# Pooled attention and a maxout layer on one core: five batches' keys turned by DMA, their copies on another engine, two schedules shifted

## The chip, the cores and the metric

The kernel runs on one core of a Trainium2 chip. The metric is the device time of one execution in microseconds, as a median over runs. The core's engines are TensorE (PE; its weight loads are listed apart as PEld), VectorE (DVE), ScalarE (ACT), GpSimd (POOL) and SyncE (SP). SP's work here is issuing DMAs; POOL and ACT can issue some as well. Each engine takes its instructions in program order and waits where a semaphore tells it to.

## The reference

```python
# attention with pooled keys and values: 8 batches, 8 heads, 576 rows, 64 columns
k_p = k.reshape(B, H, Sp, pool, D).mean(axis=3)      # pool = 8, Sp = 72
v_p = v.reshape(B, H, Sp, pool, D).mean(axis=3)
scores = np.matmul(q, k_p.transpose(0, 1, 3, 2)) / np.sqrt(D)
attn = softmax(scores)                               # over the 72 pooled keys
x = matmul(attn, v_p).transpose(0, 2, 1, 3).reshape(4608, 512)
# maxout layer
h = np.maximum(np.maximum(x @ w1, x @ w2), x @ w3)   # 512 -> 768
out = h @ w_out                                      # 768 -> 512
```

## The kernel before

The 4608 tokens are worked off in nine blocks of 512 (`block`, L432). A block has slots. A slot of `hidden_part` (L289) is one of three weight matrices for one block `jc` of 128 hidden columns: four matmuls into a PSUM tile `pw` (three buffers), which is then emptied: the first by a cast on ACT (L301), the second by a maximum on DVE (L304), the third by a maximum on DVE that writes hT (L307). Six column blocks make 18 slots. Four slots of `project` (L323) follow, each six matmuls for 128 tokens, a copy from PSUM to `osb` (five buffers) and two stores.

Between the slots stands the attention of a later batch. What comes after which slot is written out by hand: for block 0 in the dictionary at L447, for the others in `plan` (L456), and `do` (L258) carries the steps out. Block n works on batch n + 1:

- `T`: the queries are transposed into `qT` by one DMA transpose on SP's queue (L270), a block ahead. `q`/`Q` do it on PE, with the copy on ACT or DVE.
- `k` (`turn_k`, L183): the pooled keys `kp` are transposed by six PE transposes into one PSUM tile `pkt` (L174), and two copies (L179) spread them into the zero-padded `kz`, one for even heads and one for odd ones. `a` and `K` pool batch 1's keys.
- `s0` to `s7`: the scores of a head, three matmuls (L203), and their exponential on ACT (L208).
- `v0` to `v4`: a chunk of 128 tokens, eight matmuls (L238), then a reciprocal and a product on DVE (L244, L246) that give `xn`.
- `x0` to `x4`: such a chunk is transposed into `xT`, the input of `hidden_part`: by PE and a copy (L229, L233) for batches 0 and 1, by a DMA transpose on SP's queue (L223) from batch 2 on. `X` puts the copy on DVE.

Loading and pooling run on POOL: `pool_work` (L467), after the first slot of block n, issues the loads of k, q and v of batch n + 2 and adds groups of eight rows up into `kp` and `vp`. The load of k is bound to the end of the block's first group of matmuls.

As blocks 0 and 1 begin while the values of their tokens are still being worked out, `hidden` (L311) cuts their first column blocks into parts of 128 or 256 tokens.

SP's queue is the order in which the program issues: transposes `T` and `x`, and the stores. The last tile's output is made in two halves of 256 columns: ACT empties the first, DVE the second, and each half's two stores go one to SP's queue and one to ACT's.

Of the kernel before, what the change touches and what calls it, by code (L numbers as in the profile page):

```python
# [14 lines left out]
def kernel(  # L15
# [11 lines left out]
    nc = tc.nc  # L27
    dt = mybir.dt
    F32, BF16, F16 = dt.float32, dt.bfloat16, dt.float16
# [13 lines left out]
    GS = (0, 2, 4, 6, 8, 1, 3, 5, 7)  # L43
    NR = 64
    KCH = C // 128
    JCH = DFF // 128
    TOK = B * S
    NB = 512
# [4 lines left out]
    sb2 = ctx.enter_context(tc.tile_pool(name="sb2", bufs=2))  # L53
# [1 line left out]
    psp = ctx.enter_context(tc.tile_pool(name="psp", bufs=1, space=PSUM))  # L55
    ctx.enter_context(tc.manual_schedule())

    kts, vts, qbs, kps, qTs, ets = {}, {}, {}, {}, {}, {}

    def after(loads, first):  # L60
        for x in loads:
# [49 lines left out]
    for i in range(3):  # L111
# [6 lines left out]
        out=wo_sb, in_=moe_w_out.rearrange("(jc p) c -> p jc c", p=128))  # L118
# [25 lines left out]
    def fold_k(b, e, i0=0, i1=6):  # L144
        if b not in kps:
            new_kp(b)
        fold(e, kts[b][:, i0:i1], [kps[b][:, i0:i1, i, :] for i in range(2)])
# [23 lines left out]
    def keys(b, tag):  # L171
        pkt = psp.tile([128, 6, 96], BF16, name="pkt", tag=tag[0], bufs=tag[1])
        for i in range(6):
            nc.tensor.transpose(pkt[:, i, :], kps[b][:, i, :, :], ident[0:96, 0:96])  # L174
        return pkt

    def fill_kz(b, par, h0, h1, pkt, evac):
        rows = slice(64 * par, 64 * par + 64)
        evac(out=kz_all[b % 2][rows, par, h0:h1, 0:Sp].rearrange(  # L179
                 "p h (r i) -> p h r i", i=6),  # L180
             in_=pkt[rows, :, 12 * h0:12 * h1].rearrange("p i (h r) -> p h r i", r=12))

    def turn_k(b):  # L183
        pkt = keys(b, TR)
        for par in range(2):
            fill_kz(b, par, 0, H, pkt,
                    nc.scalar.copy if b == 1 else nc.vector.tensor_copy)

    def pool_k(b, tag):

# [19 lines left out]
    def new_et(b):  # L210
        ets[b] = sb2.tile([Sp, H, S], F16, name="et", tag="et")
# [40 lines left out]
    TR = ("tr", 1)  # L252
# [5 lines left out]
    def do(b, steps):  # L258

        for name in steps.split():
            i = int(name[1:] or 0)
            if name[0] in "qQ":
                turn_q(b, *QS[i], nc.vector.tensor_copy if name[0] == "Q"
                       else nc.scalar.copy, TR)
            elif name[0] == "T":
                qTs[b] = sb2.tile([128, 2 * NG, 128], BF16, name="qT", tag="qT")
                nc.sync.dma_start_transpose(  # L270
                    out=qTs[b], in_=qbs[b].rearrange("p hp t d -> p (hp t d)"))
            elif name[0] == "k":
                turn_k(b)
            elif name[0] == "K":
                pool_k(b, PW)
            elif name[0] == "a":
                nc.vector.tensor_tensor(out=k16, in0=kts[b][:, :, 0:4],
                                        in1=kts[b][:, :, 4:8], op=ALU.add)
            elif name[0] == "s":
                if i == 0:  # L280
                    new_et(b)
                scores(b, i)
            elif name[0] == "v":
                xns[b, i] = values(b, CHUNKS[i][0])
            else:
                turn_x(b, *CHUNKS[i], xns[b, i], TR,
                       nc.vector.tensor_copy if name[0] == "X" else nc.scalar.copy)
# [23 lines left out]
    def hidden(n, hT):  # L311

        parts = [(0, JCH, 0, NB)]
        if n == 0:
            parts = [(0, 1, 0, 128), (0, 1, 128, 256), (1, 2, 0, 256), (0, 2, 256, NB),
                     (2, JCH, 0, NB)]
        elif n == 1:
            parts = [(0, 1, 0, 256), (0, 1, 256, NB), (1, JCH, 0, NB)]
        for j0, j1, c0, c1 in parts:
            for jc in range(j0, j1):  # L320
                yield from hidden_part(n, jc, c0, c1, hT)

    def project(n, hT):  # L323
        for mm in range(4):
            m = 4 * n + mm
            last = m == TOK // 128 - 1
            osb = sb3.tile([128, C], F32, name="osb", tag="osb", bufs=5)
            for c in ((slice(0, C // 2), slice(C // 2, C)) if last else (slice(0, C),)):
                po = psp.tile([128, c.stop - c.start], F32, name="po", tag="pw", bufs=3)
                for jc in range(JCH):  # L330
                    nc.tensor.matmul(po, hT[:, jc, bass.ts(mm, 128)], wo_sb[:, jc, c],  # L331
                                     start=(jc == 0), stop=(jc == JCH - 1))
                if c.start:
                    nc.vector.tensor_copy(out=osb[:, c], in_=po)
                else:
                    nc.scalar.copy(out=osb[:, c], in_=po)  # L336
                for u in range(2):
                    b, g = divmod(2 * m + u, NG)
                    dst = out[S * b:S * b + S, :].rearrange("(r g) c -> r g c", g=NG)
                    (nc.scalar if last and u else nc.sync).dma_start(  # L340
                        out=dst[:, GS[g], c], in_=osb[64 * u:64 * u + 64, c])
            yield

    def new_hT():
        return sb2.tile([128, JCH, NB], F16, name="hT", tag="hT")
# [13 lines left out]
    for i in range(0, 6, 2):  # L359
        src = kts[0][:, i:i + 2] if i else kt0  # L360
        f = const.tile([96, 2, 4, D], F32, name="kf", tag="kf")
# [5 lines left out]
            out=kps[0][:, i:i + 2].rearrange("p i a d -> p a i d"),  # L367
# [64 lines left out]
    def block(n, plan):  # L432

        hT = new_hT()
        slot = 0
        for part in (hidden(n, hT), project(n, hT)):
            for _ in part:
                if slot == 0 and n > 0:
                    pool_work(n, mms[-1])
                for b, steps in plan.get(slot, ()):  # L440
                    if b < B:
                        do(b, steps)
                slot += 1

    fold_v(1)
    fold_k(2, nc.gpsimd)
    block(0, {0: [(0, "X1")], 3: [(0, "v2")], 5: [(0, "v3")], 6: [(0, "x2")],  # L447
# [6 lines left out]


    def plan(n):  # L456
        b, i = n + 1, 3 * (n == 1)
        got = {0: [], 3: [], 3 + i: [(b, "k")]}
        got.update({5 + i + h: [(b, f"s{h}")] for h in range(H)})
        got[12 + i].append((b + 1, "T"))  # L460
        got.update({15 + i + c: [(b, f"v{c} x{c}")] for c in range(5)})
        if n == 1:
            got[0].append((1, "x3"))
            got[3].append((1, "x4"))
        return got
# [45 lines left out]
```

The softmax here doesn't subtract the row's maximum and nothing guards it: scores larger than these inputs give would overflow.

## Time and profile before

| | |
|---|---|
| median of 5 runs | 243.14 us (242.5 to 245.42) |
| profiled execution | 242.5 us, its span 240.7 us |
| PE busy | 231.5 us, 1609 matmuls |
| matmuls of the hidden layer (L295) | 696, 155.6 us |
| matmuls of the projection (L331) | 222, 50.7 us |
| key transposes on PE (L174), 96 columns | 54, mean 206 ns |
| copies to kz on DVE, 64x576 | 12, mean 755 ns |
| copies to kz on ACT, 64x576 | 2, mean 633 ns |
| DMA transposes to xT on SP's queue | 30, median 2.4 us to landing (2.3 to 7.9) |
| DMA transposes to qT on SP's queue | 6, median 6.6 us to landing (4.5 to 8.1) |

The span runs from the first to the last recorded instruction; the time of an execution also holds 1.8 us around it. In the timeline a row gives start, duration, engine, line, operation, tile written and tiles read, shape, count, and in brackets how long the engine was idle before it and what ended that. A matmul's duration goes from its start to the end of its last result, so successive matmuls overlap in the record and their pace is read from their starts. A "q" after an engine's name means its instruction queue, as for DMAs that it issues.

### The profile page before, as it was taken

Reading aid. Unit: us, or ns where it says so; the run is one execution under the profiler, and the core shown is the slowest. Engines: PE = TensorE matmul, PEld = TensorE weight load, DVE = VectorE, ACT = ScalarE, POOL = GpSimd, SP = SyncE. Lnnn points to the kernel's source line nnn. Section 1 sums busy time; section 2 is a strip of 40 time slices with the busy share of each in tenths; the row PEclk is TensorE's granted clock in tenths of the full one; section 3 lists DMA queues with packets and bytes.
Section 4 is the critical chain, followed back from the end, with each engine's and each line's share of the span. In section 5 each row is a group of like instructions: output and inputs, shape, how many; then the busy total and the mean of one; then the engine's idle time right before and its main releaser. Section 6 shows DMA issues by size and latency. Waiting matters only on the chain.

```text
span 240.7 us, 4221 instructions
## 1 busy us (share of the span) xinstructions
PE 231.5 (96%) x1609; PEld 123.0 (51%) x1609; DVE 131.6 (55%) x239; ACT 100.1 (42%) x173; POOL 123.7 (51%) x91
## 2 busy tenths in 40 slices
PE   7798999999999999999999999999999999999992
PEld 2477555575554555455545554555455544444441
DVE  6856754564574558354836483648364834504530
ACT  2373347546523651365135523552355232142121
POOL 8864265999997489557953787389200000000000
PEclk9999999999999999999999999999999999999999
DMA  7999999999958994799489967997530353042006
GB/s 138 181 198 206 194 200 210 182 160 245 156 128 148 218 198 91 133 229 204 102 151 186 186 146 143 213 184 130 121 87 0 69 124 83 3 109 66 0 20 154
DMA packets 51939, 34.29 MB, mean 142 GB/s; under 512 B 32144, under 2 KB 46480, under 8 KB 51920
## 3 DMA queue, kind: packets, MB, share of 16 engines
q0 software_dynamic: 17088, 17.11, 45.7%
q1 hardware_dynamic: 34672, 16.79, 33.3%
q8 instruction: 12, 0.20, 0.3%
q10 hardware_dynamic: 160, 0.13, 0.2%
q14 instruction: 7, 0.06, 0.1%
HBM read 34.60 MB, written 9.44 MB: 183 GB/s over the span
## 4 chain that ended last, share of the span: by engine, by line
PE 88%; DVE 5%; ACT 2%; DMA 2%; issue 1%; DVEq 0%
PE pw L295 55%; PE po L331 18%; PE psc L203 6%; PE pav L238 4%; DMA kt<-in_k_dram 2%; PE pxt L229 1%; DVE kf L362 1%; ACT et L208 1%; DMA out_dram<-osb 1%; DVE t L304 1%; PE pkt L174 1%; PE pvp L156 1%; DVE xn L246 1%; PE pqt L167 1%; DVE kp L366 1%
## 5 line engine op out<-in xcount | busy, mean ns | idle before, releaser
L295 PE MATMUL pw<-xT,mw 128*128 128x512 f16 (+2 forms) x696 | 155.6, 364 | 0.7 <-ACT xT L233 0.7
L295 PEld LDWEIGHTS <-mw 128*128 128x128 f16 x696 | 61.9, 98 | 56.1 <-issue 1.0
L304 DVE TENSOR_TENSOR t<-t,pw 128x512 f16<-128x512 f16 (+2 forms) x58 | 37.8, 651 | 71.0 <-PE pw L295 43.7
L301 ACT CAST t<-pw 128x512 f16<-128x512 f32 (+2 forms) x58 | 32.3, 556 | 56.1 <-PE pw L295 54.8
L331 PE MATMUL po<-mwo,hT 128*128 128x512 f16 (+1 forms) x222 | 50.7, 373 | 0.0
L208 ACT ACTIVATE et<-psc 72x576 f16<-72x576 f32 (+2 forms) x62 | 40.7, 662 | 20.9 <-PE psc L203 20.8
L307 DVE TENSOR_TENSOR hT<-t,pw 128x512 f16<-128x512 f16 (+2 forms) x58 | 37.7, 650 | 9.0 <-PE pw L295 5.3
L336 ACT COPY osb<-po 128x512 f32<-128x512 f32 (+1 forms) x36 | 20.9, 580 | 47.7 <-PE po L331 43.6
L135 POOL TENSOR_TENSOR half<-vt 72x2048 f32<-72x2048 f16 x7 | 28.4, 4060 | 7.0 <-DMA vt<-in_v_dram 6.9
L331 PEld LDWEIGHTS <-hT 128*128 128x128 f16 x222 | 20.3, 97 | 21.3 <-DVE hT L307 2.4
L135 POOL TENSOR_TENSOR half<-kt 96x1536 f32<-96x1536 f16 x6 | 18.5, 3084 | 21.2 <-DMA kt<-in_k_dram 21.2
L246 DVE TENSOR_TENSOR xn<-pav,rcp 128x512 f16<-128x512 f32 x39 | 27.0, 691 | 1.6 <-DVE rcp L244 0.2
L136 POOL TENSOR_TENSOR half<-half 72x1024 f32<-72x1024 f32 (+1 forms) x13 | 27.3, 2098 | 1.0
L203 PE MATMUL psc<-qT,kz 128*128 128x64 bf16 (+3 forms) x192 | 25.8, 246 | 0.4 <-DVE kz L179 0.3
L203 PEld LDWEIGHTS <-kz 128*128 128x128 bf16 x192 | 17.8, 98 | 15.6 <-DVE kz L179 1.5
L238 PEld LDWEIGHTS <-et 72*128 72x128 f16 x312 | 15.2, 98 | 7.6
L238 PE MATMUL pav<-vp,et 72*128 72x65 f16 x312 | 16.5, 194 | 0.0
L244 DVE RECIPROCAL rcp<-pav 128x8 f32<-128x8 f32 x39 | 7.9, 204 | 9.4 <-PE pav L238 9.3
L139 POOL TENSOR_TENSOR kp<-half 96x384 bf16<-96x384 f32 x12 | 11.7, 993 | 0.5
L179 DVE COPY kz<-pkt 64x576 bf16<-64x576 bf16 (+1 forms) x14 | 9.9, 711 | 2.9 <-PE pkt L174 2.7
L79 POOL DMA_DIRECT2D vt<-in_v_dram x10 | 8.0, 804 | 3.9 <-PE pw L295 2.9
L139 POOL TENSOR_TENSOR vp<-half 72x512 f16<-72x512 f32 x7 | 8.9, 1269 | 0.5
(48 smaller groups left out, 79.8 us busy)
## 6 DMA issues: line engine op xcount, KB each, us to landing
out_dram<-osb SPq DMA_DIRECT2D x70, 128.0 KB, 2.4
kt<-in_k_dram POOLq DMA_DIRECT2D x7, 576.0 KB, 6.9
qb<-in_q_dram POOLq DMA_DIRECT2D x7, 576.0 KB, 11.3
vt<-in_v_dram POOLq DMA_DIRECT2D x7, 576.0 KB, 14.5
mw<-in_moe_w_dram POOLq DMA_DIRECT2D x9, 256.0 KB, 10.2
mwo<-in_moe_w_out_dram POOLq DMA_DIRECT2D x1, 768.0 KB, 18.3
qb<-in_q_dram POOLq DMA_DIRECT2D x2, 288.0 KB, 6.4
xT<-xn SPq DMA_TRANSPOSE x30, 2.4
```

What stands on the lines that cost most here:

```text
L135: e.tensor_tensor(out=f, in0=t[:, :, 0:4, :], in1=t[:, :, 4:8, :], op=ALU.add)
L136: e.tensor_tensor(out=f[:, :, 0:2, :], in0=f[:, :, 0:2, :], in1=f[:, :, 2:4, :], op=ALU.add)
L203: nc.tensor.matmul(out, kz_all[b % 2][:, f % 2, h, :], qTs[b][:, n + i0:n + i1, 64 * (h % 2):64 * (h % 2) + 64], start=True, stop=True)
L208: nc.scalar.activation(out=out, in_=in_, func=FT.Exp, scale=1.0 / 64.0)
L238: nc.tensor.matmul(pav[:, h // 4, 65 * (h % 4):65 * (h % 4) + 65], ets[b][:, h, c0:c0 + 128], vp_all[:, b, h, :], start=True, stop=True)
L246: nc.vector.tensor_tensor(out=xn, in0=pv[:, :, :, 0:D], in1=rcp.to_broadcast([128, 2, 4, D]), op=ALU.mult)
L295: mm = nc.tensor.matmul(pw, w_sb[wi][:, kc, bass.ts(jc, 128)], xT[:, kc, col], start=(kc == 0), stop=(kc == KCH - 1))
L301: nc.scalar.copy(out=t, in_=pw)
L304: nc.vector.tensor_tensor(out=t1, in0=t, in1=pw, op=ALU.max)
L307: nc.vector.tensor_tensor(out=hT[:, jc, c0:c1], in0=t, in1=pw, op=ALU.max)
L331: nc.tensor.matmul(po, hT[:, jc, bass.ts(mm, 128)], wo_sb[:, jc, c], start=(jc == 0), stop=(jc == JCH - 1))
L336: nc.scalar.copy(out=osb[:, c], in_=po)
```

## The change

Five things are edited.

1. For batches 3 to 7 a new step `Z` transposes `kp` by a DMA on SP's queue into a tile `kT` in SBUF (two buffers). `Z` of batch n + 2 is issued in block n after slot 17 (20 in block 1), behind `x3` of batch n + 1. `turn_k` then has no PE work for these batches: it copies from `kT`. Batches 1 and 2 keep PE.
2. The two copies to `kz` go to ACT for every batch but 2 (in `turn_k`; before, only batch 1's did), and for blocks 2 and later stand after slot 2 instead of 3, so three slots ahead of `s0`. In block 1 they stay after slot 6.
3. From block 1 on the value steps stand one slot earlier: `v0` after slot 14 (17 in block 1), not 15 (18).
4. In block 0 column block 2 joins column block 1 in being worked in two halves of 256 tokens. That makes three more slots, and the hand-written order is spread over them: `x2`, `x3`, `v4`, `x4`, `a`, `K`, `k` and what follows move; the first query copy goes to ACT (`q0`), and the scores are dealt out differently.
5. The last tile's two halves are both emptied by DVE. Both stores of the first half and one of the second go to ACT's queue, and one of the second to SP's.

On SP's queue the order in block n from 1 on becomes: `T`, `x0`, `x1`, `x2`, `x3`, `Z`, two stores, `x4`, six stores. It was: `T`, `x0`, `x1`, `x2`, two stores, `x3`, two stores, `x4`, four stores.

```diff
@@ turn_k
-        pkt = keys(b, TR)
+        pkt = keys(b, TR) if b < 3 else kTs[b]
         for par in range(2):
             fill_kz(b, par, 0, H, pkt,
-                    nc.scalar.copy if b == 1 else nc.vector.tensor_copy)
+                    nc.vector.tensor_copy if b == 2 else nc.scalar.copy)
@@ do
+            elif name[0] == "Z":
+                kTs[b] = sb2.tile([128, 6, 96], BF16, name="kT", tag="kT")
+                nc.sync.dma_start_transpose(
+                    out=kTs[b], in_=kps[b].rearrange("p i a d -> p (i a d)"))
@@ hidden
-            parts = [(0, 1, 0, 128), (0, 1, 128, 256), (1, 2, 0, 256), (0, 2, 256, NB),
-                     (2, JCH, 0, NB)]
+            parts = [(0, 1, 0, 128), (0, 1, 128, 256), (1, 3, 0, 256), (0, 3, 256, NB),
+                     (3, JCH, 0, NB)]
@@ project
-                if c.start:
+                if last:
                     nc.vector.tensor_copy(out=osb[:, c], in_=po)
                 else:
                     nc.scalar.copy(out=osb[:, c], in_=po)
                 for u in range(2):
                     b, g = divmod(2 * m + u, NG)
                     dst = out[S * b:S * b + S, :].rearrange("(r g) c -> r g c", g=NG)
-                    (nc.scalar if last and u else nc.sync).dma_start(
-                        out=dst[:, GS[g], c], in_=osb[64 * u:64 * u + 64, c])
+                    e = nc.scalar if last and (u or c.start == 0) else nc.sync
+                    e.dma_start(out=dst[:, GS[g], c], in_=osb[64 * u:64 * u + 64, c])
@@ block 0
-    block(0, {0: [(0, "X1")], 3: [(0, "v2")], 5: [(0, "v3")], 6: [(0, "x2")],
-              8: [(0, "x3")], 10: [(0, "v4")], 12: [(0, "x4")],
-              13: [(1, "a")], 15: [(1, "K")], 17: [(1, "k")], 19: [(1, "Q0")],
-              20: [(1, "Q1")], 21: [(1, "Q2 s0")], 22: [(1, "Q3 s1")],
-              23: [(1, "s2 s3")], 24: [(1, "s4 s5")], 25: [(1, "s6 s7")],
-              26: [(1, "v0")], 27: [(1, "v1 x0"), (2, "T")], 28: [(1, "v2 x1")],
-              29: [(1, "v3 x2")], 30: [(1, "v4")]})
+    block(0, {0: [(0, "X1")], 3: [(0, "v2")], 5: [(0, "v3")], 7: [(0, "x2")],
+              9: [(0, "x3")], 12: [(0, "v4")], 15: [(0, "x4"), (1, "a")],
+              17: [(1, "K")], 19: [(1, "k")], 21: [(1, "q0")],
+              22: [(1, "Q1")], 23: [(1, "Q2 s0")], 24: [(1, "Q3 s1")],
+              25: [(1, "s2")], 26: [(1, "s3 s4")], 27: [(1, "s5 s6")],
+              28: [(1, "s7")], 29: [(1, "v0")], 30: [(1, "v1 x0"), (2, "T")],
+              31: [(1, "v2 x1")], 32: [(1, "v3 x2")], 33: [(1, "v4")]})
@@ plan
-        got = {0: [], 3: [], 3 + i: [(b, "k")]}
+        got = {0: [], 3: [], (3 + i if n == 1 else 2): [(b, "k")]}
         got.update({5 + i + h: [(b, f"s{h}")] for h in range(H)})
         got[12 + i].append((b + 1, "T"))
-        got.update({15 + i + c: [(b, f"v{c} x{c}")] for c in range(5)})
+        got.update({14 + i + c: [(b, f"v{c} x{c}")] for c in range(5)})
+        got[17 + i].append((b + 1, "Z"))
```

More of the change, by code (lines that the diff above doesn't have):

```diff
@@ L56 @@
     ctx.enter_context(tc.manual_schedule())
-    kts, vts, qbs, kps, qTs, ets = {}, {}, {}, {}, {}, {}
+    kts, vts, qbs, kps, qTs, kTs, ets = {}, {}, {}, {}, {}, {}, {}
     def after(loads, first):
```

## The prediction

> **What bounds the kernel.** I read the page's busy shares and its chain first, then the stretches between block starts, then PE's own timeline, which gives every bubble.
>
> ```profile
> PE 231.5 (96%) x1609; PEld 123.0 (51%) x1609; DVE 131.6 (55%) x239; ACT 100.1 (42%) x173; POOL 123.7 (51%) x91
> PE 88%; DVE 5%; ACT 2%; DMA 2%; issue 1%; DVEq 0%
> ```
>
> ```profile
> 16.60:27.00 10.40, 9.19 (x108) 6.87 (x106) 7.24 (x18) 3.96 (x10) 4.39 (x6) 1.00 1.26 205
> 27.00:41.40 14.40, 13.95 (x101) 7.87 (x100) 7.32 (x14) 8.65 (x15) 8.52 (x4) 1.00 1.31 200
> 97.60:122.00 24.40, 24.40 (x168) 12.49 (x166) 13.81 (x24) 10.73 (x18) 16.69 (x10) 1.00 0.88 168
> ```
>
> The chain is PE for 88% of the span. The other three rows are stretches (length, then busy time of PE, PEld, DVE, ACT, POOL): in block 3, at 97.6 to 122.0, PE is never idle, and the granted clock is 1.00. Only the first 41 us hold idle PE.
>
> ```profile
> 20.17 1.04 PE L295 MATMUL pw<-xT,mw 128*128 128x256 f16 x8
> 21.37 0.40 PE L229 MATMUL pxt<-identh,xn 128*128 128x128 f16 x4 [0.16 <-DVE xn L246]
> 22.44 1.03 PE L295 MATMUL pw<-xT,mw 128*128 128x256 f16 x8 [0.67 <-ACT xT L233]
> 24.90 0.40 PE L229 MATMUL pxt<-identh,xn 128*128 128x128 f16 x4 [0.29 <-DVE xn L246]
> 33.08 0.44 PE L167 MATMUL pqt<-ident,qb 128*128 128x128 bf16 x5 [0.23 <-DVE qT L169]
> ...
> 125.30 0.42 PE L174 MATMUL pkt<-ident,kp 96*128 96x96 bf16 x6
> 125.56 1.89 PE L295 MATMUL pw<-xT,mw 128*128 128x512 f16 x8
> ```
>
> Starts tell PE's real pace, since a record runs past the next start: 512 columns take 0.216 us (16 in 3.45), 256 take 0.109, four 128-wide transposes 0.23, one head's scores 0.25, one chunk of values 0.26. By these the bubbles of block 0 after 20 us are 0.33 and 0.84 (at 21.4 and 22.4, waiting for chunk x3), 0.46 (24.9), 0.31 (27.2, the key fold on DVE), 0.40 (33.1) and 0.3 among the scores: 2.6 us. The last two lines price the keys: six transposes hold PE from 125.30 to 125.56.
>
> **Keys.** Per batch 3 to 7 six transposes leave PE: 5 x 0.26 = 1.30 us. Block 3 adds up with no bubble (96 x 0.216 + 5 x 0.26 + 8 x 0.25 + 0.26 = 24.3), so the whole of it comes off the path if nothing new is late.
>
> What comes in is one crossbar transpose per batch on SP's queue, and two copies on ACT. The crossbar step has no row for this shape. Four 128-wide blocks (xT) take 1.19 us of SP and land 2.4 after issue; eighteen (qT) take 2.41 and land after 4.5 at best, 8.1 at worst. For six blocks I take 1.4 and 2.7, near the four-block row; the ends are 2.4 and 8.1.
>
> When is it issued? T0 is the next block's start.
>
> ```profile
> 86.97 2.41 SPq L270 DMA_TRANSPOSE qT<-qb  x1
> 90.67 4.64 SPq L223 DMA_TRANSPOSE xT<-xn  x3
> 95.40 1.19 SPq L340 DMA_DIRECT2D out_dram<-osb  x2
> 96.68 1.25 SPq L223 DMA_TRANSPOSE xT<-xn  x1
> 98.03 1.18 SPq L340 DMA_DIRECT2D out_dram<-osb  x2
> 99.30 1.22 SPq L223 DMA_TRANSPOSE xT<-xn  x1
> ```
>
> ```profile
> xT<-xn SPq DMA_TRANSPOSE x1, 7.6
> ```
>
> This is SP's queue around T0 = 97.6; the single line, from the view of DMA issues, is the time to landing of the transpose issued at 99.30. Chunk x0 is at T0-7.0 now. The value steps move one slot earlier (0.86 + 0.26), so x0 goes to T0-8.1; x3 follows DVE (three value chunks, a maximum pair, 0.84 and 1.2 us) to about T0-4.0, and the keys behind it to T0-2.7. They land near T0. Their input is ready: POOL ends kp at 88.6 in block 2, six us before. Behind them on SP wait two stores, x4 and six stores. x4 then leaves at about T0-0.1 instead of T0+1.7 and is read only a block later; stores have five buffers. Both cost nothing.
>
> Who waits for kT? ACT reaches the two copies after its first cast, at T0+1.5, and copies from PSUM of this shape took 0.634 each (1.28 for both at 30.02), so they end at T0+2.8. ACT's next cast becomes ready at T0+3.7, so 0.9 us is left in front of it; PE needs that cast's PSUM buffer at T0+5.4. A kT landing up to T0+3.5, or copies from SBUF at twice the price, is still covered; beyond that every us is a PE bubble. DVE is rid of its two copies (1.54 us at 101.38), for which PE did not wait: zero. Queued behind ACT's wait for kT are that cast and the exponentials.
>
> The Trainium skill speaks against this part: "VectorE: DVE Perf Modes", The three transpose paths and Rules for kernel authors, gives 390 ns for a 128x128 tile on TensorE against 1309 ns by the crossbar, and prefers TensorE where PSUM will do. As an estimate, six tiles one after another would be 7.9 us, a landing at T0+5.1, 1.6 us late in five blocks: 8 us lost instead of 1.3 won. The trace's eighteen blocks in 4.5 us disagree.
>
> Value steps a slot earlier: the last hT maximum now has two full value chunks ahead of it on DVE, not one, and the projection that reads it is also one chunk (0.26) and one slot later by comparison. By DVE's row pace it ends 4.2 us after the first reciprocal, needed at 4.2; now it is 3.1 against 3.1. Equal: zero, plus or minus 0.1 in six blocks.
>
> **Block 0.** The third early half group puts 1.3 us of matmuls between x3 and its first reader. Twelve 512-wide matmuls become 24 of 256: +0.02 us. I walk PE from 19.46, up to where nothing differs, with the paces above. Three 256-wide weight passes (0.44 each) and x2 (0.23) end at 21.0. The new group's first pass ends at 21.4, and x3, whose product is ready at 21.31, follows with no bubble; its second ends at 22.1. The third needs weights issued at 12.4 that took 9.8, so it waits 0.16 and ends at 22.7. By then ACT has copied x3 (22.6). Three passes of the second halves and v4 (0.26) end at 24.3, one pass and x4 at 24.9 with its product ready at 24.5, two passes at 25.8. The fold of k, 0.95 on DVE behind two maxima, still stalls PE 0.3; the pooled sums (0.65) end at 26.75. The key transposes come two 256-wide passes (0.87) behind these, where it was two 512-wide ones (1.72), while the kp copies need 1.3 (0.55 on DVE, then 0.47 on ACT): a new bubble of 0.43. They end at 28.3, one half pass at 28.7, column block 3's first at 29.6. q0 waits 0.15 for the kz copies to free its PSUM, Q1 0.2 for q0's copy on ACT; with two passes, three query groups' worth of transposes and s0 PE reaches column block 4 at 32.7, instead of 33.35. There the weights gate it: their last third was issued at 16.8, 18.2 and 20.1 and took 16.2, 16.2 and 15.6, so it lands at 33.0, 34.3 and 35.7. The third pass of column block 4 starts at 35.75 instead of 36.02. Itself, three more passes (four times 0.86) and five heads' scores (1.25), make 4.7, and waiting for exponentials 0.15: v0 at 40.6. It is at 41.27 now, with six heads' scores behind that pass. Gain 0.65, not the 1.3 that PE's bubbles alone would give. Ends: 0.2 (another 0.4 late on ACT or DVE) and 1.3 (weights not gating).
>
> Batch 2 keeps its PE keys. Its qT, issued at 45.55 behind two stores, can start at 45.1, when qb lands, so 0.2 us of its 0.7 us of slack goes; covered.
>
> **Last tile.** SP's last store waits now: data ready at 236.75, issued 237.66, landed 239.74. SP then has one fewer store and ends near 239.0; ACT has three at 236.1, 236.8 and 237.4, and at 2.1 to 2.4 to landing (its two rows) ends at 239.5 to 239.8. Gain 0.15; ends -0.2 and +0.4.
>
> **Sum.** 1.30 + 0.65 + 0.15 = 2.1 us. The profiled execution took 242.5 (span 240.7), so 240.4; it was the fastest of five, 0.64 under the median of 243.14, so the median goes to 241.0.
>
> **Rivals.**
> The keys arrive late (slower). A transpose issued at 99.30, 1.7 us after T0, took 7.6 us to land, and a store issued 1.0 after T0 took 6.0, while one issued 0.4 after it took 2.3: the loads for a later batch start at T0+1.2. It decides if the key transpose leaves SP later than about T0+0.4. Then kT lands near T0+8.5, ACT stands, and PE loses 5 us in each of blocks 2 to 5, where loads run: about 261. In block 2 alone (qT held by its load, 65.9, then four chunks, so T0-1.6) it is 5 - 2.1, so 246. For it: that thin place. Against: 2 to 3 us of margin. Chance 0.12, mostly the single block.
> The early group gains nothing, since weights, fold and kp copies stand in turn: 1.3 + 0.1, so 241.7. The landings speak for it. Chance 0.17.
> The weights land earlier than in this execution and the tail gives its upper end: 1.3 + 1.3 + 0.4 = 3.0, so 240.1. Chance 0.08.
> My sum: 0.63.
>
> **Numbers.** The forecast's own ends are 1.3 - 0.1 + 0.2 - 0.2 = 1.2 and 3.0, so 241.9 to 240.1, and half a us of spread of the median: 239.8 to 242.6 holds all but the late keys. About 1% (2.4 us) is what a measurement here can tell from no change. The forecast of 2.1 lies just inside: a quarter of its 0.63 beyond, plus 0.08 and spread, faster 0.28; slower 0.12; within 0.60.
>
> **What would show it.** Block 3 should be 24.0 us with no pkt row, kz copies on ACT, and nothing waiting for kT. The 0.67 before the first matmul at columns 256 should go, and a wait at L174 appear; v0 of batch 1 near 40.6. A kT wait on ACT over 2 us, or time to landing of kT above 5, makes the prediction wrong; so would a bubble at L331 behind hT.

## The result, and the profile after

| | before | after |
|---|---|---|
| median | 242.96 us (80 executions, 242.43 to 245.44) | 241.89 us (43 executions, 240.26 to 244.61) |
| ratio after to before | | 0.9952, 95% interval 0.994 to 0.9965 |
| fastest | 242.43 | 240.26 |
| profiled execution | 242.5, span 240.7 | 242.95, span 241.1 |

The change gains 1.1 us in the median, half of the forecast 2.1, and 2.2 us between the fastest executions. So the saving is there, and most executions give part of it back; the spread has grown with it.

The page of after, busy shares and chain, to set against the first two lines shown of before:

```profile
PE 231.1 (96%) x1591; PEld 123.7 (51%) x1591; DVE 123.4 (51%) x231; ACT 112.0 (46%) x184; POOL 123.7 (51%) x91
...
PE 85%; DVE 4%; DMA 4%; issue 2%; ACT 2%; SPq 1%; POOL 0%; DVEq 0%; POOLq 0%
```

ACT carries 12 us more and DVE 8 us less. On the chain DMA has 4% where it had 2%, and SP's queue, which was absent, 1%. Of DMA's share 2.8% is the load of the first queries and 1.0% the key transposes.

The stretches of after from block start to block start (length, then busy time of PE, PEld, DVE, ACT, POOL, granted clock, DMA share, GB/s), blocks 0, 1, 2, 3, 6:

```profile
18.74:49.55 30.81, 29.91 (x291) 20.05 (x288) 18.71 (x41) 16.48 (x34) 18.98 (x13) 1.00 1.20 195
49.55:74.31 24.76, 24.76 (x192) 14.11 (x189) 14.88 (x28) 11.59 (x21) 23.20 (x13) 1.00 0.91 171
74.31:98.47 24.16, 24.16 (x162) 12.21 (x160) 12.16 (x22) 13.07 (x20) 16.68 (x11) 1.00 0.95 162
98.47:122.50 24.03, 24.03 (x161) 12.29 (x161) 12.16 (x22) 13.07 (x20) 16.61 (x10) 1.00 0.97 176
...
170.53:195.02 24.49, 24.17 (x161) 12.27 (x160) 12.15 (x22) 12.96 (x20) 1.66 (x2) 1.00 0.43 82
```

Block 6 of before, cut at rounded times:

```profile
170.50:194.80 24.30, 24.30 (x168) 12.49 (x166) 13.89 (x24) 10.73 (x18) 0.00 (x0) 1.00 0.35 77
```

Block 3 is 24.03 where it was 24.4. Block 6 is 24.49 and PE is idle in it for 0.32 us, which it was not before. And block 0 starts at 18.74, where before's started at 16.71: this execution was late before any edited instruction was reached, which is most of why its 242.95 is above the median.

Block starts read off PE's timeline in the same way give the following table for every kernel profiled. "Blocks 2-6" is the sum over the five; T1 is the start of block 1, and so on; T alone is the start of the block whose scores need the keys spoken of.

| kernel | time | start of block 0 | block 0 | block 1 | blocks 2-6 |
|---|---|---|---|---|---|
| before | 242.50 | 16.71 | 31.73 | 24.75 | 121.47 |
| after | 242.95 | 18.74 | 30.82 | 24.76 | 120.71 |
| after again (e4) | 242.14 | 16.82 | 30.86 | 25.17 | 121.30 |
| keys on PE (e3) | 244.55 | 19.60 | 30.81 | 24.76 | 121.36 |
| early key transpose (e2) | 243.81 | 20.10 | 30.81 | 24.76 | 120.08 |
| copies on DVE (e1) | 244.56 | 20.93 | 30.82 | 24.76 | 120.08 |
| strided writes (e5) | 249.16 | 19.28 | 30.81 | 24.76 | 126.30 |
| late key transpose (e6) | 266.80 | 17.39 | 30.82 | 25.54 | 145.09 |
| early and DVE (e7) | 242.57 | 17.00 | 30.81 | 26.52 | 120.33 |
| the same, longer warm-up (e8) | 240.83 | 17.27 | 30.82 | 24.76 | 120.08 |
| after, longer warm-up (e9) | 242.64 | 17.32 | 30.82 | 26.56 | 120.08 |
| before, longer warm-up (e10) | 245.63 | 19.87 | 31.73 | 24.75 | 121.47 |
| e8, batch 2 a slot later (e11) | 240.96 | 17.10 | 30.82 | 25.12 | 120.07 |
| e8, loads of batch 3 later (e12) | 240.74 | 17.01 | 30.82 | 24.76 | 120.24 |

The edits to block 0 and to the keys are paid in full wherever nothing comes late: 30.82 for 31.73, and 120.08 for 121.47. Three columns vary from execution to execution: the start, block 1 and blocks 2 to 6. The rest of this part is about what stands behind the last two.

**Where block 6 loses.** SP's queue in after around its start, 170.53 (T6):

```profile
159.96 4.46 SPq L270 DMA_TRANSPOSE qT<-qb  x1
164.50 6.39 SPq L223 DMA_TRANSPOSE xT<-xn  x4
170.98 1.22 SPq L274 DMA_TRANSPOSE kT<-kp  x1
172.30 1.18 SPq L345 DMA_DIRECT2D out_dram<-osb  x2
```

The query transpose holds the queue until T6-6.1. The four chunks then leave back to back, one of them taking 2.45 us instead of 1.22, and the key transpose leaves at T6+0.46, not at T6-2.7. It lands 2.4 us later, at 173.39. ACT after that, and PE:

```profile
171.59 0.59 ACT L305 CAST t<-pw 128x512 f16<-128x512 f32 x1 [0.28 <-PE pw L299]
173.41 2.36 ACT L179 COPY kz<-kT 64x576 bf16<-64x576 bf16 x2 [1.24 <-DMA kT<-kp]
175.80 0.59 ACT L305 CAST t<-pw 128x512 f16<-128x512 f32 x1
```

```profile
175.71 0.41 PE L203 MATMUL psc<-qT,kz 128*128 128x320 bf16 x3
176.44 1.02 PE L299 MATMUL pw<-xT,mw 128*128 128x512 f16 x4 [0.32 <-ACT t L305]
```

The bracket on the copies is the wait for kT, 1.24 us. The two copies take 2.36, not 1.27, so the cast behind them begins at T6+5.27; PE needs the PSUM buffer that this cast empties, and stands for 0.48 us between matmul starts. The landing was 2.9 us after T6, inside the 3.5 that the prediction called covered for copies of 0.63 us each.

The group of these copies on the page:

```profile
L179 ACT COPY kz<-kT 64x576 bf16<-64x576 bf16 x10 | 11.7, 1170 | 2.7 <-DMA kT<-kp 2.6
```

Against 633 ns for ACT's copy of this shape out of PSUM, the mean is 1170 ns.

**A smaller loss at the start of block 3.** In after, e7 and e12 the first matmul of block 3 comes 0.14, 0.27 and 0.16 us late. It starts 0.25 us after chunk x2 has landed, and in all three x2 left SP at T3-2.6, behind a query transpose that landed only at T3-2.7. In before x2 left at T3-3.8.

### The profile page after: what moved, and what is told of

Read it like the earlier page. It is cut to its first block, busy times and chain, and to the rows that moved or that the text cites. A ratio compares the mean times of both kernels' runs of the same rounds, so it can differ in the third digit from the quotient of the medians.

```text
span 241.1 us, 4202 instructions
## 1 busy us (share of the span) xinstructions
PE 231.1 (96%) x1591; PEld 123.7 (51%) x1591; DVE 123.4 (51%) x231; ACT 112.0 (46%) x184; POOL 123.7 (51%) x91
## 3 DMA queue, kind: packets, MB, share of 16 engines
q0 software_dynamic: 17088, 17.11, 45.1%
## 4 chain that ended last, share of the span: by engine, by line
PE 85%; DVE 4%; DMA 4%; issue 2%; ACT 2%; SPq 1%; POOL 0%; DVEq 0%; POOLq 0%
PE pw L299 53%; PE po L335 17%; PE psc L203 7%; PE pav L238 4%; DMA qb<-in_q_dram 3%; DVE xn L246 1%; SPq L223 1%; PE pqt L167 1%; ACT kz L179 1%; DMA kT<-kp 1%; PE pxt L229 1%; PE pvp L156 1%; PE wm L356 1%; DVE hT L311 1%; POOL kt L72 0%
## 5 line engine op out<-in xcount | busy, mean ns | idle before, releaser
L299 PEld LDWEIGHTS <-mw 128*128 128x128 f16 x708 | 62.9, 98 | 55.0 <-issue 1.3
L335 PE MATMUL po<-mwo,hT 128*128 128x512 f16 (+1 forms) x222 | 49.6, 373 | 0.0
L340 ACT COPY osb<-po 128x512 f32<-128x512 f32 x35 | 20.5, 586 | 46.0 <-PE po L335 44.6
L203 PE MATMUL psc<-qT,kz 128*128 128x64 bf16 (+3 forms) x192 | 26.4, 250 | 0.3 <-DVE kz L179 0.3
L179 ACT COPY kz<-kT 64x576 bf16<-64x576 bf16 x10 | 11.7, 1170 | 2.7 <-DMA kT<-kp 2.6
## 6 DMA issues: line engine op xcount, KB each, us to landing
mwo<-in_moe_w_out_dram POOLq DMA_DIRECT2D x1, 768.0 KB, 17.5
```

The lines of the kernel that those rows point to most:

```text
L203: nc.tensor.matmul(out, kz_all[b % 2][:, f % 2, h, :], qTs[b][:, n + i0:n + i1, 64 * (h % 2):64 * (h % 2) + 64], start=True, stop=True)
L299: mm = nc.tensor.matmul(pw, w_sb[wi][:, kc, bass.ts(jc, 128)], xT[:, kc, col], start=(kc == 0), stop=(kc == KCH - 1))
```

## The experiments

**e4, after again.** No edit; the changed kernel beside the next three on one chip, where before had a median of 242.82 (35 executions).

> The changed kernel itself, beside the others on the same chip. 241.9 in the median; a second profile of it. Theory A: blocks 2 to 6 with a kT landing later than 2.4 us after the block's start are longer than 24.0 by that excess, the others are not. Theory B: the first hidden matmul starts near 18.7 again.

Median 242.3 (240.41 to 245.6, 12 executions), ratio 0.9967 (0.994 to 0.9993). The profiled execution started on time and shows both weak places. ACT and PE at T6 = 168.90:

```profile
172.56 2.34 ACT L179 COPY kz<-kT 64x576 bf16<-64x576 bf16 x2 [2.01 <-DMA kT<-kp]
174.92 0.58 ACT L305 CAST t<-pw 128x512 f16<-128x512 f32 x1
```

```profile
174.08 0.30 PE L203 MATMUL psc<-qT,kz 128*128 128x320 bf16 x1
174.95 0.29 PE L203 MATMUL psc<-qT,kz 128*128 128x192 bf16 x2 [0.57 <-ACT kz L179]
175.56 1.02 PE L299 MATMUL pw<-xT,mw 128*128 128x512 f16 x4 [0.32 <-ACT t L305]
```

The keys landed at T6+3.6, and block 6 lost 1.22 us: the second head waits for the second copy, and the next group for the cast. In the same execution they landed at T4+1.8 and T5+1.9 at no cost. With T6+2.9 costing 0.48 in after, the limit is near T+2.4. That is the T+5.4 at which, by the prediction, PE needs the buffer, less 2.36 for the copies and 0.59 for the cast. It is theory A; theory B fails here, since this execution started at 16.82 and lost all the same. Block 1 lost 0.42 to another transpose, that of batch 2's queries.

**e3, the keys back on PE.** Everything else of the change stays.

```diff
-        pkt = keys(b, TR) if b < 3 else kTs[b]
+        pkt = keys(b, TR)
...
-                    nc.vector.tensor_copy if b == 2 else nc.scalar.copy)
+                    nc.scalar.copy if b == 1 else nc.vector.tensor_copy)
...
-        got = {0: [], 3: [], (3 + i if n == 1 else 2): [(b, "k")]}
+        got = {0: [], 3: [], 3 + i: [(b, "k")]}
...
-        got[17 + i].append((b + 1, "Z"))
```

> The changed kernel with the keys of batches 3 to 7 on PE as before (no key transpose by DMA, copies on DVE after slot 3); the value steps one slot earlier, block 0 and the last tile as changed. Theory A: block 0 and the tail alone, 0.8 to 1.1 us under the kernel before, about 242.0, with runs as close together as those of the kernel before. Theory B: the late start costs its us here as well, so 242.9 to 243.1.

Median 242.35 (241.72 to 244.55), ratio 0.9979 (0.9955 to 1.0002). Its block 3:

```profile
99.45:123.72 24.27, 24.27 (x168) 12.52 (x167) 13.64 (x24) 10.71 (x18) 16.33 (x10) 1.00 1.00 167
```

It has 168 matmuls, after's block 3 161, and is 0.24 us longer; five such blocks are 121.36 against 120.08, so the keys are worth 1.28. No bubble appears after 50 us, so the value steps a slot earlier cost nothing. Block 0 keeps its 0.9. The median lies 0.6 above the fastest execution, with no keys on DMA, so late keys are not all that spreads the times. Between the fastest executions e3 is 0.80 under before (242.52), and e4 1.3 under e3.

**e2, the key transpose earlier.** It goes behind chunk x2 in blocks 1 and 2, and behind x1 from block 3, instead of behind x3; ACT still copies.

```diff
-        got[17 + i].append((b + 1, "Z"))
+        got[16 + i - (n > 2)].append((b + 1, "Z"))
```

> The changed kernel with the key transpose one place earlier on SP's queue (behind x2) in blocks 1 and 2 and two places (behind x1) from block 3 on; copies on ACT as in the changed kernel. Theory A: kT lands 1.3 to 2.6 us earlier, so under 2.4 us after the block's start everywhere, and the time is 240.8 to 241.2. Theory B: 241.9.

Median 241.35 (240.45 to 244.58), ratio 0.9942 (0.9911 to 0.9973), 0.95 under e4 on the same chip, though the two intervals overlap. The keys land between T-1.1 and T+1.1, the copies still take 1.17 each, and blocks 2 to 6 are 24.01 or 24.02 each. For these blocks putting the landing right is enough; the slow copies are then covered.

**e1, the copies on DVE.**

```diff
-                    nc.vector.tensor_copy if b == 2 else nc.scalar.copy)
+                    nc.scalar.copy if b == 1 else nc.vector.tensor_copy)
```

> The changed kernel with the copies from kT on DVE instead of ACT; all else the same. Theory A (the missing us is lost in blocks 2 to 6: the copies take 1.17 us each on ACT, so ACT has 2.4 us before it is late, and kT lands between 0.3 and 2.9 us after the block's start): the loss goes away, 1.9 to 2.4 us under the kernel before, about 240.8, and the runs lie closer together; blocks 2 to 6 all 24.0 us even where kT lands at 2.9. Theory B (the missing us is lost ahead of the first hidden matmul, which stood at 18.7 us in the profile of the changed kernel and at 16.7 before): no different from the changed kernel, 241.9, as wide.

```profile
L179 DVE COPY kz<-kT 64x576 bf16<-64x576 bf16 x10 | 6.4, 645 | 0.2
```

DVE copies the same tile in 645 ns and starts only at T+3.40; the keys landed as late as T4+2.8 and T6+2.8, and blocks 2 to 6 are again 120.08. So the other remedy suffices as well. The median, 243.17 (240.41 to 246.12), says nothing of the keys: 7 of the 12 executions had a mean granted clock of 0.991 or less, and the profiled one started block 0 at 20.93. The fastest three, 240.41 to 240.74, stand with after's. The ratio of 0.9951 (0.9916 to 0.9987) is wide for this reason.

**e5, ACT reads kT in its order.** Is it the stride of the read that doubles ACT's copy? The edit turns the loop of the copy around, so that the read is contiguous and the write is strided.

```diff
+                nc.scalar.copy(
+                    out=kz_all[b % 2][rows, par, :, 0:Sp].rearrange(
+                        "p h (r i) -> p i h r", i=6),
+                    in_=pkt[rows].rearrange("p i (h r) -> p i h r", r=12))
```

> The changed kernel, but ACT's two copies from kT to kz read kT in the order in which it lies (six blocks of 96 columns) and write kz with a stride, where they read with a stride of 96 and wrote in order. Theory A (the stride of the read is what makes a copy 1.17 us instead of the 0.634 from PSUM): the copies take 0.6 to 0.7 us each, ACT is through with both 1.0 us earlier, so a kT landing up to about 3.4 us after the block's start is covered; an execution with kT no later than T0+2.9 shows no bubble in blocks 2 to 6, and the median falls by 0.3 to 0.7 us against the changed kernel, to about 241.4. Theory B (ACT's copy from SBUF costs this whatever its order, 64x576 at two bytes): 1.15 to 1.2 us each again, the time as before, 241.9 to 242.3. Theory C (a strided write of two bytes costs more than a strided read): over 1.3 us each, and 0.3 or more slower than the changed kernel.

```profile
L188 ACT COPY kz<-kT 64x576 bf16<-64x576 bf16 x10 | 21.2, 2123 | 0.6 <-DMA kT<-kp 0.4
```

Theory C, and more than it said: 2123 ns a copy, 248.77 us (246.78 to 249.91, 6 executions), ratio 1.0212 (1.0162 to 1.0262). Turned around, ACT's copy is slower still, so the kernel's order was the better of these two. The keys landed at T+0.3 to T+2.0 and blocks 2 to 5 still took 25.19: 4.27 us of copies delay the second head and the cast as a late landing would. Why the copy takes 1170 ns from SBUF and 633 from PSUM stays open: from PSUM it reads with the same stride, so the stride alone is no answer, and what a contiguous read and write would cost was not tried.

**e6, the key transpose later.** The rival of late keys, made to happen: one slot later, behind x4 too.

```diff
-        got[17 + i].append((b + 1, "Z"))
+        got[18 + i].append((b + 1, "Z"))
```

> The changed kernel with the key transpose one slot later, so on SP's queue behind chunk x4 as well, which puts it at about T0+1.5 to T0+2.6 (T0: the next block's start), after the loads of a later batch have started at T0+1.2. The prediction's rival of late keys says that it lands near T0+8.5 where loads run (blocks 2 to 5), so each of these blocks is 5 to 6 us longer, by bubbles in front of the score matmuls that wait for ACT, and block 6, without loads, 1 to 3 us longer: 262 to 268 us in all. If the loads don't slow this transpose (six blocks of 96, 1.2 us at SP), it lands 2.3 us after issue, T0+3.8 to T0+5, and by the threshold of T0+2.4 each of five blocks loses 1.4 to 2.6 us: 249 to 255. If instead ACT has cover up to T0+3.5, as the prediction said, 242 to 250.

266.8 us in its one execution. From the view of the tile kT, and ACT in block 3 (T3 = 104.40):

```profile
  DMA kT<-kp: 24.7, 5
...
DMA to landing us min/median/max: 2.4/5.4/10.0
```

```profile
105.47 0.59 ACT L305 CAST t<-pw 128x512 f16<-128x512 f32 x1 [0.28 <-PE pw L299]
115.97 2.35 ACT L179 COPY kz<-kT 64x576 bf16<-64x576 bf16 x2 [9.91 <-DMA kT<-kp]
```

The transposes left SP at T+0.5 to T+2.2. One issued at T3+1.5, behind the loads that start at T+1.3, took 10.0 us to land; one at T2+0.5 took 7.2, one at T4+0.8 5.4; one at T5+0.5 took 2.4, as did that of block 6, where nothing is loaded. Blocks 2, 3 and 4 lost 6.6, 10.3 and 5.5 us. That is 1.2 to 1.7 more than their landings lie past T+2.4, and the clock had fallen to half while PE stood, which fits the excess. Block 3, where PE resumed at 117.18:

```profile
117.00:121.00 4.00, 2.87 (x9) 1.18 (x10) 1.38 (x2) 2.54 (x5) 2.94 (x3) 0.50 1.14 198
```

Blocks 5 and 6 landed at T+2.8 and T+4.6 and lost 0.4 and 2.2, as the limit of T+2.4 asks. The cliff is real and lies about where the rival put it, but it is no sharp edge: of two issued at T+0.5 with loads behind them one took 7.2 us and one 2.4, and in e1 one issued at T4+0.44 took 2.4. After's transposes left at T3+0.05 and T4-0.17: close, but not over it.

**e7, early keys and DVE copies together.** e2's and e1's edits.

> Key transpose behind x2 (blocks 1 and 2) and behind x1 (from block 3), and its copies to kz on DVE from batch 3 on. If lateness of kT and the ACT copies are the only things that kept the changed kernel from the forecast, either remedy alone suffices and both together give nothing more: blocks 2 to 6 of 24.01 to 24.02 us each, fastest executions 240.3 to 240.6, median 240.5 to 241.3 depending on how many executions start late. If the copies on DVE come between the maxima of the late chunks and their readers, a bubble shows there and blocks are longer than 24.1: 241.5 or more.

Median 241.8 (240.6 to 244.91), ratio 0.9933 (0.9897 to 0.997): no more than e2, as either remedy suffices, and above the 240.5 to 241.3 that was expected. Blocks 3 to 6 are 24.01 or 24.02, block 2 is 24.28 for its late chunk, and block 1 took 26.52. From the view of tile qT between 40 and 60 us:

```profile
L270 SPq DMA_TRANSPOSE qT<-qb x1: 4679/4679/4679, 45.0 to 45.0; - x1
...
  PE psc L203: 1.6, 1
...
DMA to landing us min/median/max: 10.5/10.5/10.5
```

It was issued at T1-2.8, landed at T1+7.65 and kept the first score matmul of batch 2 waiting; block 1 is 1.77 over its 24.75. With e4 (landing T1+6.30, 0.42 over) and e6 (T1+6.67, 0.79 over) this gives a limit of T1+5.88, past which every us is lost. Before's own landed at T1+5.22.

**e8, the same with a longer warm-up.** 22 matmuls ahead of the first data instead of 17.

```diff
-    heat(17)
+    heat(22)
```

> The same as the run before it, with 22 warm-up matmuls on PE instead of 17, so that PE idles for less time between the last of them and the first transpose of queries, which waits for qb. Theory: an idle time beyond about 2.5 us there halves the granted clock for some 4 us, which costs 2 to 4 us in the executions where the loads of q come late, so with the longer warm-up no execution has a mean clock under 0.993 (in the changed kernel about one in eight had), and the spread between the fastest and the median shrinks to 0.5 us or less: median 240.4 to 240.9. Rival: the clock has nothing to do with it, the late load itself costs the time; then the median and spread are those of the run before it, 240.5 to 241.3. Should the warm-up now end after qb has landed at its earliest, executions with an early landing lose up to 0.9 us: fastest 241.2 instead of 240.4.

Median 240.87 (240.51 to 243.12), ratio 0.9925 (0.9898 to 0.9952), the lowest median of all: 1.97 under before's 242.84 beside it. One execution of 12 had a clock under 0.993. The chain of its page, and its block 6:

```profile
PE 91%; DVE 4%; DMA 2%; ACT 1%; issue 1%; DVEq 0%
```

```profile
168.90:192.91 24.01, 24.01 (x162) 12.25 (x160) 13.35 (x24) 10.71 (x18) 1.86 (x2) 1.00 0.41 80
```

This is the forecast's profile: no bubble above 0.06 us after 40 us. How much of the step from e7 is the warm-up and how much the draw of 12 executions, the intervals can't tell; e9 and e10 ask.

**e9, after with the longer warm-up, and e10, before with it.** The one-line edit of e8 in each.

> The changed kernel with 22 warm-up matmuls in place of 17, nothing else. Theory: two things kept the changed kernel's median 1.5 us above its fastest execution: late starts with a halved clock, which the longer warm-up removes, and keys that land too late for ACT's copies, which it leaves. So few executions under a mean clock of 0.993 (at most 2 of 12), fastest 240.4 to 240.7, and a median of 241.2 to 241.8, that is 0.3 to 0.9 above that of the kernel with early keys on DVE and the same warm-up (240.87). Rival (only the start matters): median 240.7 to 241.0. Rival (only the keys matter): 241.9 to 242.3 as without it.

> The kernel before with 22 warm-up matmuls in place of 17. Its own median lies only 0.3 us above its fastest execution, with 3 to 4 of 23 to 35 executions late by 2 to 4 us, so the longer warm-up should do next to nothing to the median: 242.5 to 242.9, with the tail above 244 gone. If the warm-up were worth half a us or more by itself (242.2 or less), the gain of the kernel with early keys, DVE copies and longer warm-up would have to be split otherwise.

e9: 241.78 (241.41 to 245.67), ratio 0.9938 (0.9909 to 0.9968). e10: 242.98 (242.61 to 245.63), ratio 0.9989 (0.9953 to 1.0024). For before the warm-up does nothing that can be told from noise, and 2 of 12 executions were late all the same, the profiled one among them. e9's median lies in the band of the theory, but its profile doesn't bear the reason out: the keys cost nothing (landings of T+0.6 to T+2.1, blocks 2 to 6 120.08), and the fastest execution missed by 0.7. What it lost stands in block 1, in PE's timeline:

```profile
52.33 1.89 PE L299 MATMUL pw<-xT,mw 128*128 128x512 f16 x8
55.87 0.41 PE L203 MATMUL psc<-qT,kz 128*128 128x320 bf16 x3 [1.64 <-DMA qT<-qb]
```

The queries landed at T1+7.70, and block 1 is 1.81 over: by the limit of T1+5.88 it should be 1.82.

**e11, batch 2 a slot later.** e8 with every step of batch 2 in block 1 moved on by one slot.

```diff
-        b, i = n + 1, 3 * (n == 1)
+        b, i = n + 1, 4 * (n == 1)
```

> The kernel with early keys, copies on DVE and the longer warm-up, and with every step of batch 2 in block 1 one slot later (scores from slot 9, not 8). Theory: the faster block 0 moved the deadline of batch 2's query transpose up by 0.9 us to 5.9 us after block 1's start, while its issue is held at 45.0 by the load of its input; it takes 5 to 10.5 us to land, and in two profiles block 1 was longer by exactly what the landing passed 5.9. One slot later gives it 0.9 us back: block 1 is 24.75 unless qT lands later than T1+6.8, the executions at full clock above 241.5 (2 of 12 before) become at most 1 of 12, and the median falls by 0.1 to 0.3, to 240.6 to 240.8. Rival: the later x2 and keys of batch 2 come late at block 2's start, which shows as a bubble there, and the fastest execution is 240.9 or more.

Median 241.27 (240.96 to 243.22), ratio 0.9918 (0.9884 to 0.9953). Its block 1 is 25.12 although the queries landed at T1+2.6:

```profile
54.72 0.30 PE L203 MATMUL psc<-qT,kz 128*128 128x320 bf16 x1
55.20 0.28 PE L203 MATMUL psc<-qT,kz 128*128 128x192 bf16 x2 [0.19 <-DVE kz L179]
```

The edit moved the keys of batch 2 as well, and DVE's copies now end too late for the second head: 0.35 us in this execution. That is near what its fastest execution lies above the others. The rival foresaw the fastest execution, but put the wait at block 2's start, where there is none; neither named this one, so the run doesn't decide between them.

**e12, the loads of batch 3 later.** e8 with the loads, and the pooling behind them, three slots later in block 1.

```diff
-                if slot == 0 and n > 0:
+                if n > 0 and slot == 3 * (n == 1):
```

> The kernel with early keys, copies on DVE and 22 warm-up matmuls (240.87 when it ran), with the three loads of batch 3 (and the pooling of batch 2's values behind them on POOL) issued three slots, some 2.6 us, later in block 1, at about T1+3.8 in place of T1+1.2. Theory: where the query transpose of batch 2 is still under way when these loads start (four profiles with the early start: issued at 45.0 to 46.1, loads from 48.9 to 49.3), it takes 8.1 to 10.5 us to land, and otherwise 4 to 6.5; with the loads later it lands within 6.5 us in the profile and block 1 is 24.7 to 24.8, also with a start before 17.5, fastest 240.4 to 240.6, median 240.6 to 240.9, no execution at full clock over 241.5. Rival (the load of batch 2's values, up to 49 to 50, is what delays it): landings of 8 to 10 us remain, with block 1 longer by what passes T1+5.9, and a median of 240.9 to 241.8. If the later loads hold up batch 2's values or batch 3's keys instead, a bubble shows in block 1 or 2 behind POOL's work or ACT and DVE waiting for it, and the fastest execution is above 240.9.

Median 241.39 (240.56 to 244.87), ratio 0.9941 (0.9914 to 0.9968). In the profile the queries land 6.2 us after issue, at T1+3.4, and block 1 is 24.76, as the theory asks; but e8 and e11 had 5.4 and 5.5 with the loads in their old place, and the median is that of the rival, with executions of 242.72 and 242.94 at mean clocks of 0.996 and 1.00. Also the edit did less than was meant: the loads began at T1+2.4, not at T1+3.8, and the load of batch 2's values had ended at 48.88, before they would have begun without the edit. So the loads of batch 3 are not shown to be the cause.

## Why the prediction was half right

**The sum held where nothing comes late.** Forecast 1.30 + 0.65 + 0.15; in profiles 1.39 (keys, with a bubble of 0.10 that before's block 3 happened to have), 0.9 (block 0) and 0.0 (tail). It is 2.3 of saving against 2.1, and the fastest executions differ by 2.2. Two errors of opposite sign, 0.25 in block 0 and 0.15 in the tail, nearly cancel in it. That the median of 241.9 lies in the range is the doing of the range's width: it got there by late transfers, for which the sum had put nothing.

**Block 0** was mis-sized, 0.9 for 0.65. Much of the walk was right: the bubbles at x3 and x4 are gone, and the wait at L174 stands where it was put, 0.44 between starts for a forecast 0.43. Not in it were a wait of 0.23 for DVE 3.4 us into the block and 0.5 in place of 0.3 at the pooled sums. PE's timeline of after:

```profile
28.39 0.81 PE L194 MATMUL pkp<-k,identh 96*128 96x384 f16 x4 [0.33 <-DVE k L281]
29.04 1.04 PE L299 MATMUL pw<-xT,mw 128*128 128x256 f16 x8
30.36 0.43 PE L174 MATMUL pkt<-ident,kp 96*128 96x96 bf16 x6 [0.28 <-ACT kp L197]
```

Off was the gate of the weights. PE was to reach column block 4 at 15.99 us after the block's start and then wait, so that the third pass came at 19.04, as the last weights landed. PE reached it at 16.43, in e4 and in after alike, and the third pass came at 18.91 and 18.88, with no bubble in front. The weights did not set this: the last of them landed 18.86 us after the block's start in e4, but 16.49 in after, 2.4 us ahead of the pass. So it is PE's own pace, and as PE came 0.4 later than in the walk, the upper end of 1.3 "weights not gating" was not reached either. From there to v0 it was 4.77 for 4.85. So v0 came 23.64 to 23.68 us after the start, for 23.89. The rival in which this group gains nothing has fallen.

**The tail** gave nothing, for a forecast 0.15. The last landing did come earlier, 3.25 us after PE's end for 3.45. But before the program ends SP waits for its outstanding transfers one after another, at 0.06 us each. In before one more such wait follows the one that the last landing ends; in after five do, and the span ends 4.47 us after PE's end, as before (4.45).

**The keys: the step that failed is "the keys behind it to T0-2.7".** It put x0 at T0-8.1, 1.1 us ahead of before. Two things were wrong with it. The first is DVE. Block 6 has no query transpose in the queue, and its first value chunk shows the step, in before (T7 = 194.67) and in after (T7 = 195.02):

```profile
186.91 0.21 DVE L244 RECIPROCAL rcp<-pav 128x8 f32<-128x8 f32 x1 [0.44 <-PE pav L238]
```

```profile
186.14 0.69 DVE L311 TENSOR_TENSOR hT<-t,pw 128x512 f16<-128x512 f16 x1
186.74 0.20 DVE L244 RECIPROCAL rcp<-pav 128x8 f32<-128x8 f32 x1
```

In before DVE waited for the chunk. In after the chunk's matmuls start one slot, 0.86 us, earlier (T7-9.1 for T7-8.2), but its reciprocal stands behind a maximum without a gap. So x0 left at T7-7.3 where it had left at T7-6.8: 0.5 us came forward, not 1.1. In block 1 it was the same, and the keys left at T2-2.1.

The second is SP's queue, where the query transpose stands in front. The working took its shortest issue, the 2.41 us of the row that it showed; the other five of before took 3.1 to 4.6, and after's 3.4 to 5.3, most of them starting when their input lands. In blocks 2 to 5 x0 left only at T-6.5 to T-6.0, later than before's T-6.8 to T-6.7, and the keys left at T+0.05, T-0.2, T-1.3 and T+0.5. In the five blocks that took 0.6 to 3.2 us of the margin.

The rest of the margin was a price. A landing "up to T0+3.5, or copies from SBUF at twice the price" was called covered, and each by itself is, as far as it was tried: landings up to T+2.8 with quick copies in e1, slow copies with landings up to T+1.1 in e2. Both at once came true and are not covered (after's block 6, e4's). Where the limit is passed, each us of delay is a us of PE.

Of the signs that the prediction named, block 3 near 24.0, the wait at L174 and v0 near 40.6 (40.50 in e4) came. The sign "nothing waiting for kT" did not: ACT waited 2.6 us in all in after, and in e4's block 6 2.01 at once, just over the 2 us that were to make the prediction wrong.

The crossbar's price was right. The taken 1.4 of queue and 2.7 to landing are 1.22 and 2.3 to 2.4 in all five rows of after. The Trainium skill ("VectorE: DVE Perf Modes", The three transpose paths) gives 1309 ns for one 128x128 tile, by which the estimate was 7.9 us; for several tiles in one transpose the measurement decides: six blocks of columns held the queue for 1.22 us, as long as four did.

**The thin place in block 2** was named for the keys, and after's keys were nowhere over the edge. In e6 the price beyond it, put at 5 us, was 5.5 to 10.3 in three blocks and 0.4 in the fourth. The place that costs time was batch 2's queries, which the prediction called covered: "0.2 us of its 0.7 us of slack goes". It let the landing move with the issue. The issue did move, to 45.1 in e4 and 45.0 in e7; the landing did not, 54.0 and 55.5 where before's was at 53.7, while the deadline came forward with block 0, from 54.3 to 53.6 and 53.7.

**What the median lost.** After's executions lie on average further from their fastest than before's: 1.6 us from fastest to median, for 0.5. Late keys are part of it: 0.5 and 1.2 us in block 6 of after and of e4, though nothing in e9, and nothing in any profile with early keys or with copies on DVE. The medians point the same way, e4 242.3 and e2 241.35 beside it, but not beyond their intervals. Late queries of batch 2 are another part: 0.4 to 1.8 us in four profiles (e4, e6, e7 and e9) of the six with the change that started before 17.5 and have the loads in their old place. Late chunks at block 3's start are a third, of 0.3 us at most. The shares in the whole set can't be given, since only the profiled executions show their inside. Open stays what makes these queries land 5.4 or 10.5 us after issue. In the profiles that started on time, before's among them, the landings of 8 us and more are the five where the load of batch 2's values ended at 49.4 to 50.0, after the next loads had begun at 48.9 to 49.3; in the two where it ended by 48.0 they took 5.4 and 5.5. That is an order of events in seven executions, and e12 did not settle which of them matters.

The version to keep is e8 (early key transpose, copies on DVE, longer warm-up), with the lowest median; its interval overlaps those of e2, e7, e11 and e12, which share the early transpose, and e11's ratio of 0.9918 is lower still.

## What to carry to other kernels

Before a step is moved ahead on an in-order DMA queue, take the longest issue time seen of each transfer in front of it, and ask whether the queue or the producer sets its departure. A margin that holds for a late input or for a dearer operation, each by itself, has to be tried for both at once. When a part gets faster, every transfer whose landing is set by something else loses the same time of slack: look for its deadline there.

## What was not expected of the hardware

- **ACT's copies of two-byte data.** The same 64x576 copy took 633 ns from PSUM and 1170 from SBUF, both with a strided read, and 2123 from SBUF with a strided write; DVE took 645 from SBUF with the strided read (e1).
- **The clock after an idle start.** PE waits for q after its warm-up. Between starts the wait was 1.46 us in before and 2.27 in e6, and the clock stayed at 1.00. It was 2.32 in e3, 2.55 in e10, 2.65 in e1, 2.70 in after, 3.38 in e2 and 3.66 in e5, and the clock went to half, between 0.3 us before work resumed and 1.9 us after it, for 3.4 us (6.8 in e1). e10, columns as in the stretches above:

```profile
10.00:11.00 1.00, 0.51 (x9) 0.52 (x10) 0.23 (x2) 0.00 (x0) 0.28 (x1) 1.00 1.15 179
11.00:12.00 1.00, 0.71 (x16) 0.56 (x14) 1.00 (x3) 0.78 (x2) 0.47 (x1) 0.90 1.28 186
12.00:13.00 1.00, 1.00 (x5) 0.65 (x6) 0.27 (x1) 0.50 (x2) 0.25 (x1) 0.50 1.36 193
```

  It was back at full by 16, and block 0 started at 19.87 instead of 16.71; 2.0 of the 3.2 us are the later q, whose first transpose stands at 10.49 for 8.51. The Trainium skill ("TensorE: Matmul & The Clock Gate", The HAM clock gate) gives one idle window of some 3.4 us, of a window that runs freely, as what drops the clock; here 2.32 us were enough. Five more warm-up matmuls did not keep e10 from it, since q landed late by more than they filled.
- **A DMA transpose under loads.** The same six blocks took 2.4 us to land in all of after, 3.7 to 4.4 once each in seven other runs (e2, e5, e7, e8, e9, e11, e12), and 5.4 to 10.0 three times in e6, when issued 0.5 to 1.5 us after a block's start, shortly before or behind the loads.
